# Attention features, a softplus layer and a gated layer in one kernel: two pairs of weight buffers in place of four shared ones, and another pool for the tile y

## The chip, the cores and the metric

The kernel runs on one core of a Trainium2 chip. The metric is device time in microseconds of one execution, the median of the runs shown. The core has five engines that run side by side, each through its own queue in order: TensorE (PE in the profile, its weight loads PEld), VectorE (DVE), ScalarE (ACT), GpSimd (POOL) and SyncE (SP), which here only starts DMAs. They wait for one another by semaphores.

## What is computed

Three layers follow each other, all in float32 (shapes of the reference: batch 4, 8 heads, sequence 576, head size 64, so 2304 tokens of 512):

```python
q_p, k_p = phi(q * scale), phi(k * scale)          # 128 random features each
kv = einsum('bhsm,bhsd->bhmd', k_p, v); z = sum(k_p, axis=2)
x = (q_p @ kv) / (q_p @ z + 1e-6)                  # -> 2304 x 512
h = x @ w_in                                       # 512 -> 2048
g = maximum(h, 0) + log1p(exp(-abs(h)))            # softplus
y = g @ w_out                                      # 2048 -> 512
out = (((y @ w1) * (y @ w2)) @ w3) @ w_out2        # 512 -> 1024 -> 1024 -> 512
```

The five weight matrices come in as 64-bit floats; the kernel makes 32-bit floats of them on the chip, out of the two words of each.

## The kernel before

**Split products.** A float32 product is made of three matmuls of rounded operands (`mm3`, L89): hi by hi, hi by lo and lo by hi, where hi is the rounded value (a copy on ACT) and lo the rest (a subtraction on DVE or POOL). All matmuls are of line L87.

**Stages.** First the attention features (0 to about 150 us). Then *Up1*, the first wide stage (150 to about 341 us): x @ w_in with softplus, in 24 quads. A quad (class `Quad`, L450) is one weight block `win[i]` by one of three groups of 768 tokens; seven products of 384 columns stand for eight, and the sums of operands are made beforehand: s1 to s4 of the tokens (`operands`, L409) and t1 to t4 of the weights (`sum_13`, `sum_2`, `sum_4`). The products are added up by DVE (`add`, L475) out of PSUM, whose banks PE needs again for the next quad: the product with s1 is the third of a quad. Then *pass 1* (about 341 to 598 us): g @ w_out (`down`, L565) in five chunks of tokens (512 four times, then 256), the first two together, so that 16 rows f of w_out times two chunks make 32 steps of 12 matmuls. During pass 1 eight products w3 @ w_out2 are made as well, one each three steps from step 42 on (`fold`). Then *Up2*, the second wide stage, and *pass 2*, the last product.

**The stream of pass 1.** A step m loads `dn` four steps ahead (SP's queue), splits it two steps ahead into `dhi` (ACT, L581) and `dlo` (DVE, L582) and multiplies. At the end of a chunk four accumulators are copied out as `y` (`evict_down`, L614: d = 1, 3 on ACT at L618, d = 0, 2 on DVE at L620), and `store_y` (L732) puts their stores into a list `late`, which `before_1` issues on SP's queue at the start of the next step that isn't the first of a chunk. At the first boundary two chunks end, so there are eight y. Operands `dn`, `dhi`, `dlo` and `y` all come from `mt()`: the pool M_, 14 buffers.

**Weight conversion.** A weight block is a `Job` (L112). Its steps: `load` (DMA on ACT's queue into one of two buffers of L_), `relu` (ACT, L127, takes the buffer f), `floor`, `bits_a`, `bits_b`, `bits_c` (DVE, L130, L136, L143, L150), and then the splits: `hi_` (ACT, L176) and `lo_` (POOL, L181) of f. Blocks with `sums` (w_in and w1/w2) also make t from f (DVE, L157, L160, L163) and split it, `hi_t` (ACT, L189) and `lo_t` (POOL, L193), ahead of f. Four of the w1/w2 blocks are `kept`: their f is stored to DRAM (`spill`, from ACT's queue) in pass 1 and read back in Up2 (`reload`). f, t and the token sums s1 to s4 all come from `tt()`: the pool T_, four buffers under one tag. The splits go to J_ (eight slots) or to X0 and X1, pools of 14 and 28 slots under the tag "x", which hold the token operands of a wide stage (14 per group) and in pass 1 the split w_out blocks (the first 7 in X0, the last 4 in X1, two slots each) and 7 split blocks of w_out2 (X1).

**What sets the order.** Program order is written out by hand: a list `queue` of conversion steps from which `step(rate)` takes some after each product or step of a pass; `need` and `until` take more where PE needs the result. A step that takes slots of J, X0 or X1 waits in the list until the counter `free[pool]` allows it; these counters are bookkeeping in the program text only. The framework then fixes the order of each engine's queue when the program is built: it runs a model of the machine, starts what is ready, program order being the priority (less `URGENT` = 300 for additions, evictions and the stream's splits), and a tile gets a buffer of its pool and tag when one is free in that model. On the chip each engine follows its fixed order and waits where the earlier user of a buffer isn't done.

Of the kernel before, what the change touches and what calls it, by code (L numbers as in the profile page):

```python
# [19 lines left out]
F32 = mybir.dt.float32  # L20
# [24 lines left out]
N = 384  # L45
# [17 lines left out]
def body(ctx: ExitStack, tc: tile.TileContext, q, k, k_rest, v, v_rest, om_t, w_in, w_out, w12, w3, wo, out):  # L63
# [2 lines left out]
    sm = ctx.enter_context(tc.tile_pool(name="sm", bufs=5))  # L66
    M_ = ctx.enter_context(tc.tile_pool(name="M_", bufs=14))
    L_ = ctx.enter_context(tc.tile_pool(name="L_", bufs=2))
    T_ = ctx.enter_context(tc.tile_pool(name="T_", bufs=4))
    J_ = ctx.enter_context(tc.tile_pool(name="J_", bufs=8))  # L70
    dr = ctx.enter_context(tc.tile_pool(name="dr", bufs=1, space=DRAM))
    ps_ = ctx.enter_context(tc.tile_pool(name="ps_", bufs=8, space=PSUM))
# [4 lines left out]
    def mt(n=512, dt=F32, name="m"):  # L77
        return M_.tile([128, n], dt, tag="m", name=name)
# [1 line left out]
    def jt(name):  # L80
        return J_.tile([128, 1024], FR, tag="j", name=name)

    def tt(name):
        return T_.tile([128, 1024], F32, tag="t", name=name)

    def matmul(o, a, b, start, stop, **kw):
        nc.tensor.matmul(out=o, lhsT=a, rhs=b, start=start, stop=stop, **kw)  # L87
# [15 lines left out]
    free = {"J": 8, "X0": 14, "X1": 28}  # L103

    def take(pool, n):
        def ok():
            return free[pool] >= n

        return ok


    class Job:  # L112
# [10 lines left out]
            return self.raw.bitcast(dt).rearrange("p (n w) -> p n w", w=2)[:, :, i]  # L123

        def relu(self):
            self.f = tt("f")[:, :self.n]
            nc.scalar.activation(out=self.f, in_=self.words(1, F32), func=AF.Relu, scale=-1.0)  # L127

        def floor(self):
# [23 lines left out]
            )  # L153

        def sum_13(self):
            self.t = tt("t")
            nc.vector.tensor_tensor(out=self.t[:, 0:512], in0=self.f[:, 256:768], in1=self.f[:, 0:512], op=ALU.subtract)  # L157

        def sum_2(self):
# [6 lines left out]
            nc.scalar.dma_start(out=self.kept, in_=self.f)  # L166

        def reload(self):
            self.f = tt("f")
            nc.sync.dma_start(out=self.f, in_=self.kept)  # L170

        def hi_(self):
# [69 lines left out]
    def until(done):  # L242
        while not done():
            assert pump_one()
# [161 lines left out]
    def xslot(pool, n, dt, name):  # L406
        return pools[pool].tile([128, n], dt, tag="x", name=name)

    def operands(c, src, pool):  # L409

        o, a, s = {}, [], {}

        def load(kk):
            def op():
                r = L_.tile([128, 2, 2 * N], F32, tag="l", name="xq")
                nc.sync.dma_start(out=r, in_=src[:, 2 * kk:2 * kk + 2, 2 * N * c:2 * N * (c + 1)])
                a.append([r[:, :, 0:N], r[:, :, N:2 * N]])
            return op

        def total(name, x, y, op_):  # L420
            def op():
                s[name] = tt(name)[:, 0:2 * N].rearrange("p (k t) -> p k t", k=2)
                nc.vector.tensor_tensor(out=s[name], in0=x(), in1=y(), op=op_)
            return op

        def parts(name, x):
            def op_hi():
                free[pool] -= 2
                o[name] = [xslot(pool, 2 * N, FR, f"x{name}{w}").rearrange("p (k t) -> p k t", k=2) for w in "hl"]
                nc.scalar.copy(out=o[name][0], in_=x())  # L430

            def op_lo():
                nc.vector.tensor_tensor(out=o[name][1], in0=x(), in1=o[name][0].bitcast(F32), op=ALU.subtract)

            return [(op_hi, take(pool, 2)), op_lo]

        a11, a21 = lambda: a[0][0], lambda: a[0][1]
        a12, a22 = lambda: a[1][0], lambda: a[1][1]
        ops = [load(0), load(1)]
        ops += parts("a11", a11)  # L440
        ops += [total("s1", a21, a22, ALU.add), total("s2", lambda: s["s1"], a11, ALU.subtract)]
        ops += parts("s2", lambda: s["s2"])
        ops += [total("s3", a11, a21, ALU.subtract)]
        ops += parts("s3", lambda: s["s3"]) + parts("s1", lambda: s["s1"]) + parts("a12", a12)
        ops += [total("s4", a12, lambda: s["s2"], ALU.subtract)]
        ops += parts("a22", a22) + parts("s4", lambda: s["s4"])
        ops.append(lambda: ready.add(c))
        return o, ops
# [89 lines left out]
    def widen(kind, jobs, after, before_last):  # L538
        n = len(jobs)
        order = [(0, 0), (1, 0), (0, 1), (0, 2), (1, 1), (1, 2)]  # L540
        order += [(i, c) for i in range(2, n - 2) for c in range(NC)]
        order += [(n - 2, 0), (n - 2, 1), (n - 1, 0), (n - 1, 1), (n - 2, 2), (n - 1, 2)]
        last_i, last_c = {i: m for m, (i, c) in enumerate(order)}, {c: m for m, (i, c) in enumerate(order)}
        quads = {}
        for m in range(len(order) + 1):
            if m < len(order):
                i, c = order[m]
                until(lambda: c in ready and jobs[i].done)
                quads[m] = kind(i, c, FIRST_RATE if m < 4 else UP_RATE)
                quads[m].begin()  # L550
            if m == len(order) - 1:
                before_last()
            if m:
                quads.pop(m - 1).finish()
                i, c = order[m - 1]
                if last_i[i] == m - 1:
                    free["J"] += 4
                if last_c[c] == m - 1:
                    free["X0" if c == 0 else "X1"] += 14
                    after(c)  # L560
# [51 lines left out]
        yield  # L612

    def evict_down(d, src, n, name):  # L614
        o = mt(n, name=name)
        with tc.high_priority(URGENT):
            if d % 2:
                nc.scalar.copy(out=o, in_=src)  # L618
            else:
                nc.vector.tensor_copy(out=o, in_=src)  # L620
        return o
# [82 lines left out]
    for s in range(NW):  # L704
        n = min(WB, NF * 512 - WB * s)
# [26 lines left out]
    def store_y(d, t0, n, src):  # L732
        y = evict_down(d, src, n, "y")
        late.append(lambda: nc.sync.dma_start(out=yd[:, d, t0:t0 + n], in_=y))
# [24 lines left out]
            queue.extend(job_ops(wout))  # L759

    widen(Up1, win, after_1, lambda: next(d1))
    ready.clear()
    for x, f in zip(w12_k, wf[KEEP:]):
        x.kept = f
# [4 lines left out]
    next(d1)  # L769
    while late:  # L770
        late.pop(0)()
    for x in wout:
        if x not in given:
            free[x.pool] += 2
# [29 lines left out]
    def store_out(d, t0, n, src):  # L804
        nc.sync.dma_start(out=out[128 * d:128 * d + 128, t0:t0 + n], in_=evict_down(d, src, n, "o"))
# [77 lines left out]
```

## Time and profile before

| | before |
|---|---|
| median of 3 runs | 881.78 us (880.67 to 882.65) |
| the profiled execution | 882.83 us |
| its span, first to last instruction | 881.0 us |
| PE busy | 850.9 us (97%), 5496 matmuls |
| DVE / ACT / POOL busy | 597.6 / 381.8 / 177.9 us |
| mean granted TensorE clock | 0.994 |
| DMA | 141.68 MB, mean 161 GB/s |

A profile is of one execution. Start times are in us from the first instruction. In a timeline row the columns are start, duration, engine, line, operation, out<-in, shape and count; in brackets stands how long the engine had been idle before it and what ended that. The granted clock is a share of 2.4 GHz. Of the profiled execution 1.8 us lie outside its span.

### The profile page before, as it was taken

To read this page: it belongs to the slowest core of one execution; us is meant where nothing else is said; L and a number is where in the kernel's file an instruction comes from. 1 tells how busy PE (TensorE), PEld (TensorE's weight loads), DVE (VectorE), ACT (ScalarE), POOL (GpSimd) and SP (SyncE) were. 2 spreads that over 40 slices of the span, in tenths; PEclk is the share of its full clock that TensorE was granted. 3 is DMA by queue.
4 is the path that set the end of the run, shared out by engine and by line. 5 is a ranking of instruction groups with operands and counts; after the bars stand their busy time and mean duration, and the time that the engine had idled before them with its cause. 6 is when DMAs were issued, how large, how long until landed. Compare 5 with 4: busy or idle time off the path is not lost.

```text
span 881.0 us, 14617 instructions
## 1 busy us (share of the span) xinstructions
PE 850.9 (97%) x5496; PEld 763.9 (87%) x5496; DVE 597.6 (68%) x932; ACT 381.8 (43%) x796; POOL 177.9 (20%) x110
## 2 busy tenths in 40 slices
PE   8999989999899999999989999999999999999998
PEld 7888878989899988788768888899999999988887
DVE  5678788888775587887986686169986655563322
ACT  6678978563443455444433332164321111132221
POOL 3524420022222243222311211100042222000000
PEclk9999999999999999999989999999999999999999
DMA  8623534565443457766676664064322211364432
GB/s 298 240 84 97 156 99 133 186 215 181 156 149 133 150 195 266 239 190 237 203 275 235 238 219 161 31 204 137 126 102 78 78 54 55 128 201 144 143 120 96
DMA packets 72535, 141.68 MB, mean 161 GB/s; under 512 B 7056, under 2 KB 39952, under 8 KB 69392
## 3 DMA queue, kind: packets, MB, share of 16 engines
q1 hardware_dynamic: 65984, 102.99, 35.0%
q10 hardware_dynamic: 6480, 37.75, 12.5%
q8 instruction: 43, 0.70, 0.3%
q14 instruction: 28, 0.23, 0.1%
HBM read 94.05 MB, written 46.66 MB: 160 GB/s over the span
## 4 chain that ended last, share of the span: by engine, by line
PE 53%; DVE 4%; DMA 2%; issue 1%; ACT 1%; POOL 0%; ACTq 0%; DVEq 0%; POOLq 0%
PE ps L87 53%; DMA raw<-in_w 1%; DVE f L150 1%; DMA dn<-gd 1%; DVE f L143 1%; DVE dlo L582 0%; DVE f L130 0%; DMA raw<-in_wo 0%; DVE f L136 0%; ACT dhi L581 0%; DVE c L475 0%; DVE u L475 0%; ACT hi L176 0%; POOL tlo L193 0%; ACT f L127 0%
## 5 line engine op out<-in xcount | busy, mean ns | idle before, releaser
L181 POOL TENSOR_TENSOR lo<-f,hi 128x512 fp32r<-128x512 f32 (+3 forms) x58 | 93.2, 1621 | 195.1 <-ACT hi L176 162.5
L582 DVE TENSOR_TENSOR dlo<-dn,dhi 128x512 fp32r<-128x512 f32 (+1 forms) x120 | 89.0, 752 | 62.6 <-ACT dhi L581 44.1
L87 PE MATMUL ps<-dlo,hi 128*128 128x512 f32 (+1 forms) x320 | 120.8, 378 | 4.8 <-DVE dlo L582 4.8
L87 PE MATMUL ps<-dhi,hi 128*128 128x512 f32 (+1 forms) x320 | 119.1, 375 | 1.2 <-DVE c L475 0.7
L87 PE MATMUL ps<-dhi,lo 128*128 128x512 f32 (+1 forms) x320 | 120.2, 376 | 0.0
L193 POOL TENSOR_TENSOR tlo<-t,thi 128x1024 fp32r<-128x1024 f32 x16 | 39.7, 2478 | 301.6 <-ACT thi L189 195.5
L581 ACT CAST dhi<-dn 128x512 fp32r<-128x512 f32 (+1 forms) x120 | 67.3, 577 | 65.5 <-DVE dlo L582 30.7
L87 PEld LDWEIGHTS ps<-dlo,hi 128*128 128x128 f32 x320 | 60.8, 190 | 17.7 <-DVE dlo L582 6.2
L130 DVE SCALAR_TENSOR_TENSOR f<-raw,f 128x1024 f32<-128x1024 f32 (+2 forms) x43 | 51.0, 1188 | 33.2 <-ACT f L127 33.0
L87 PEld LDWEIGHTS ps<-dhi,hi 128*128 128x128 f32 x320 | 60.5, 189 | 14.6 <-DVE c L475 1.8
L475 DVE TENSOR_TENSOR c<-ps,u 128x384 f32<-128x384 f32 x144 | 71.6, 550 | 0.9
L87 PEld LDWEIGHTS ps<-dhi,lo 128*128 128x128 f32 x320 | 60.9, 190 | 11.7
L482 ACT COPY p<-ps 128x384 f32<-128x384 f32 x48 | 22.9, 477 | 103.8 <-PE ps L87 99.1
L475 DVE TENSOR_TENSOR u<-ps,p 128x384 f32<-128x384 f32 x48 | 26.6, 555 | 60.8 <-PE ps L87 60.8
L127 ACT ACTIVATE f<-raw 128x1024 f32<-128x1024 f32 (+2 forms) x43 | 42.5, 993 | 49.7 <-DMA raw<-in_w 25.4
L176 ACT CAST hi<-f 128x1024 fp32r<-128x1024 f32 (+2 forms) x42 | 38.5, 922 | 57.6 <-PE ps L87 30.8
L507 ACT ACTIVATE c<-c 128x384 f32<-128x384 f32 x72 | 35.2, 524 | 63.3 <-DVE c L475 59.0
L309 DVE TENSOR_REDUCE nmax<-ps 128x4 f32<-128x512 f32 x72 | 48.2, 683 | 19.4 <-PE ps L87 10.0
L87 PE MATMUL ps<-dlo,w34h 128*128 128x512 f32 (+1 forms) x160 | 59.6, 373 | 0.0
L87 PE MATMUL ps<-dhi,w34l 128*128 128x512 f32 (+1 forms) x160 | 59.6, 373 | 0.0
L87 PE MATMUL ps<-dhi,w34h 128*128 128x512 f32 (+1 forms) x160 | 59.1, 373 | 0.0
L150 DVE SCALAR_TENSOR_TENSOR f<-raw,f 128x1024 int32<-128x1024 int32 (+2 forms) x43 | 53.1, 1236 | 0.6
(147 smaller groups left out, 2163.5 us busy)
## 6 DMA issues: line engine op xcount, KB each, us to landing
gd<-c SPq DMA_DIRECT2D x96, 192.0 KB, 2.4
dn<-gd SPq DMA_DIRECT2D x64, 256.0 KB, 3.6
raw<-in_w ACTq DMA_DIRECT2D x16, 1024.0 KB, 6.0
pd<-c SPq DMA_DIRECT2D x48, 192.0 KB, 1.9
dn<-pd SPq DMA_DIRECT2D x32, 256.0 KB, 3.2
raw<-in_w_out ACTq DMA_DIRECT2D x10, 768.0 KB, 4.1
raw<-in_w_in ACTq DMA_DIRECT2D x6, 1024.0 KB, 5.0
rawq<-in_q SPq DMA_DIRECT2D x18, 256.0 KB, 3.8
```

Source lines behind the costliest of these rows:

```text
L87: nc.tensor.matmul(out=o, lhsT=a, rhs=b, start=start, stop=stop, **kw)
L127: nc.scalar.activation(out=self.f, in_=self.words(1, F32), func=AF.Relu, scale=-1.0)
L130: nc.vector.scalar_tensor_tensor(out=self.f, in0=self.words(1, F32), scalar=SMALLEST, in1=self.f, op0=ALU.max, op1=ALU.max)
L150: nc.vector.scalar_tensor_tensor(out=fi, in0=self.words(0, I32), scalar=29, in1=fi, op0=ALU.logical_shift_right, op1=ALU.bitwise_or,)
L176: nc.scalar.copy(out=self.hi, in_=self.f)
L181: nc.gpsimd.tensor_tensor(out=self.lo[:, a:b], in0=self.f[:, a:b], in1=self.hi[:, a:b].bitcast(F32), op=ALU.subtract)
L193: nc.gpsimd.tensor_tensor(out=self.tlo, in0=self.t, in1=self.thi.bitcast(F32), op=ALU.subtract)
L309: nc.vector.tensor_reduce(out=nmax, in_=pj, axis=AX.X, op=ALU.max, negate=True)
L475: nc.vector.tensor_tensor(out=z, in0=bank, in1=y, op=ALU.add)
L507: nc.scalar.activation(out=dst, in_=src, func=AF.Softplus)
L581: nc.scalar.copy(out=hi, in_=got[m])
L582: nc.vector.tensor_tensor(out=lo, in0=got.pop(m), in1=hi.bitcast(F32), op=ALU.subtract)
```

## The change

T_ has two buffers under each of two tags in place of four under one: f takes "f", t takes "t"; of the token sums s1 and s3 take "f", s2 and s4 "t". At the end of a chunk of pass 1 y is allotted in X1, not in M_; the outputs of pass 2 stay in M_. The counter of X1 is lowered by 6 after Up1 and raised by 6 after pass 1.

```diff
-    T_ = ctx.enter_context(tc.tile_pool(name="T_", bufs=4))
+    T_ = ctx.enter_context(tc.tile_pool(name="T_", bufs=2))
...
-    def tt(name):
-        return T_.tile([128, 1024], F32, tag="t", name=name)
+    def tt(name, tag):
+        return T_.tile([128, 1024], F32, tag=tag, name=name)
...
         def relu(self):
-            self.f = tt("f")[:, :self.n]
+            self.f = tt("f", "f")[:, :self.n]
...
         def sum_13(self):
-            self.t = tt("t")
+            self.t = tt("t", "t")
...
         def reload(self):
-            self.f = tt("f")
+            self.f = tt("f", "f")
...
         def total(name, x, y, op_):
             def op():
-                s[name] = tt(name)[:, 0:2 * N].rearrange("p (k t) -> p k t", k=2)
+                s[name] = tt(name, "f" if name in ("s1", "s3") else "t")[:, 0:2 * N].rearrange("p (k t) -> p k t", k=2)
...
     def evict_down(d, src, n, name):
-        o = mt(n, name=name)
+        o = xslot("X1", n, F32, name) if name == "y" else mt(n, name=name)
...
     widen(Up1, win, after_1, lambda: next(d1))
+    free["X1"] -= 6
     ready.clear()
...
     next(d1)
     while late:
         late.pop(0)()
+    free["X1"] += 6
```

## Rows read from the trace of the kernel before

**Rows 1.** The page: its span, and the engines' busy time with the share of the span.

```profile
span 881.0 us, 14617 instructions
...
PE 850.9 (97%) x5496; PEld 763.9 (87%) x5496; DVE 597.6 (68%) x932; ACT 381.8 (43%) x796; POOL 177.9 (20%) x110
```

**Rows 2.** Windows: length, busy PE, PEld, DVE, ACT, POOL, granted clock, DMA share, GB/s.

```profile
150.00:345.00 195.00, 182.91 (x1021) 178.95 (x1022) 147.02 (x221) 93.85 (x167) 48.00 (x25) 0.99 0.52 176
345.00:445.00 100.00, 95.05 (x404) 75.06 (x402) 83.95 (x101) 46.85 (x74) 26.49 (x16) 0.99 0.69 225
...
450.00:500.00 50.00, 50.00 (x216) 40.28 (x215) 37.32 (x39) 16.60 (x24) 5.63 (x2) 1.00 0.61 210
```

**Rows 3.** Timeline of PE: the five matmuls with over 1.5 us of idle before them.

```profile
230.08 0.45 PE L87 MATMUL ps<-xs1h,thi 128*128 128x384 f32 x1 [2.30 <-DVE c L475]
...
263.07 0.44 PE L87 MATMUL ps<-xs1h,thi 128*128 128x384 f32 x1 [1.55 <-DVE c L475]
...
287.13 0.44 PE L87 MATMUL ps<-xs1h,thi 128*128 128x384 f32 x1 [1.95 <-DVE c L475]
...
311.16 0.44 PE L87 MATMUL ps<-xs1h,thi 128*128 128x384 f32 x1 [1.92 <-DVE c L475]
...
444.95 0.79 PE L87 MATMUL ps<-dlo,hi 128*128 128x512 f32 x1 [4.30 <-DVE dlo L582]
```

**Rows 4.** Timeline of ACT, 253 to 284 us: relus that had waited for POOL.

```profile
253.35 1.13 ACT L127 ACTIVATE f<-raw 128x1024 f32<-128x1024 f32 x1 [1.60 <-POOL tlo L193]
...
277.24 0.90 ACT L127 ACTIVATE f<-raw 128x768 f32<-128x768 f32 x1 [1.60 <-POOL tlo L193]
...
283.32 0.90 ACT L127 ACTIVATE f<-raw 128x768 f32<-128x768 f32 x1 [3.07 <-POOL lo L181]
```

**Rows 5.** Timeline of POOL, 256 to 284 us: the splits "lo" of two w_in blocks.

```profile
256.72 3.84 POOL L181 TENSOR_TENSOR lo<-f,hi 128x256 fp32r<-128x256 f32 x2 [3.40 <-ACT hi L176]
...
280.38 2.90 POOL L181 TENSOR_TENSOR lo<-f,hi 128x256 fp32r<-128x256 f32 x2 [3.17 <-ACT hi L176]
```

**Rows 6.** Timeline of DVE, 278 to 288 us: conversion and additions of one round.

```profile
278.17 0.96 DVE L130 SCALAR_TENSOR_TENSOR f<-raw,f 128x768 f32<-128x768 f32 x1 [2.69 <-ACT f L127]
...
280.75 1.38 DVE L150 SCALAR_TENSOR_TENSOR f<-raw,f 128x768 int32<-128x768 int32 x1
...
284.25 0.96 DVE L130 SCALAR_TENSOR_TENSOR f<-raw,f 128x768 f32<-128x768 f32 x1 [1.65 <-ACT f L127]
...
286.06 1.48 DVE L475 TENSOR_TENSOR c<-ps,u 128x384 f32<-128x384 f32 x3
```

**Rows 7.** Timelines of DVE, ACT and SP at the first boundary of pass 1.

```profile
432.79 0.68 DVE L620 COPY y<-ps 128x512 f32<-128x512 f32 x1
...
438.05 2.99 DVE L130 SCALAR_TENSOR_TENSOR f<-raw,f 128x1024 f32<-128x1024 f32 x1
...
444.21 1.28 DVE L582 TENSOR_TENSOR dlo<-dn,dhi 128x512 fp32r<-128x512 f32 x2
...
438.28 1.14 ACT L581 CAST dhi<-dn 128x512 fp32r<-128x512 f32 x2
...
442.26 6.53 SPq L574 DMA_DIRECT2D dn<-gd  x5
```

**Rows 8.** DMA issues: queue, count, KB each, median us from issue to landing.

```profile
wf<-f ACTq DMA_DIRECT2D x4, 512.0 KB, 6.8
...
yd<-y SPq DMA_DIRECT2D x16, 256.0 KB, 5.8
```

**Rows 9.** Windows again (columns as in Rows 2): the end of Up1, and after the boundary.

```profile
313.00:345.00 32.00, 31.25 (x174) 29.87 (x174) 26.68 (x39) 17.17 (x31) 14.07 (x7) 1.00 0.67 224
...
445.00:450.00 5.00, 5.00 (x12) 3.94 (x13) 3.39 (x4) 3.11 (x5) 2.37 (x1) 0.50 0.93 336
```

**Rows 10.** Timelines of ACT and POOL in pass 1: a relu, and the next split.

```profile
469.45 1.13 ACT L127 ACTIVATE f<-raw 128x1024 f32<-128x1024 f32 x1 [4.25 <-DMA raw<-in_w]
...
475.78 2.40 POOL L181 TENSOR_TENSOR lo<-f,hi 128x1024 fp32r<-128x1024 f32 x1 [27.90 <-ACT hi L176]
```

## The prediction

> **What bounds the kernel now.** I read the engines' busy time first: PE (TensorE) is busy 850.9 of 881.0 us, DVE 68%, ACT 43% [rows 1]. The time is therefore PE's own work and the holes in it. A table by stage says where holes are: in 150 to 345 us PE is busy 182.91 of 195, in 345 to 445 us 95.05 of 100, while 450 to 500 us is full at 216 matmuls, 0.2315 us apart [rows 2]. Third, PE's timeline. The reader should see five holes over 1.5 us [rows 3]: four in the first wide stage (Up1), all before the first product of "s1" and all ended by the DVE line that adds the partial products (L475), and one of 4.30 us at 444.95 in the first narrow pass, ended by "dlo" (L582).
>
> What stands behind the holes is read from the engines that run late. In Up1 the weight conversion and PE's additions share DVE's queue, which runs in order. At 253.35 ACT's relu, which opens the buffer of a weight block, had waited 1.60 us for POOL's "tlo"; at 277.24 the same again; at 283.32 it waited 3.07 us for POOL's "lo" [rows 4]; the pair returns at 301.28 and 307.35. Both are waits for a buffer of the pool T_: POOL was still reading the values or the sums in it. "lo" ended at 256.72 + 3.84 = 260.56 and at 280.38 + 2.90 = 283.28 [rows 5]. DVE's floor, next after the relu, then idles 2.69 and 1.65 us, and the additions behind it start at 286.06 [rows 6], so PE waits 1.95 us at 287.13. The hole at 230.08 has no T_ wait behind it, and I leave it.
>
> At 440.65 (444.95 less 4.30) PE has finished the first two chunks and needs the operand "dlo" of the third. Its "dhi" began at 438.28, yet "dlo" ran at 444.21, behind a floor of 2.99 us and more conversion; meanwhile "dn" loads went out from 442.26 only [rows 7]. All of dn, dhi, dlo and the eight y tiles come from the 14 buffers of M_: four dn ahead, one in use and three pairs make eleven, which leaves three for eight y; each y gives its buffer back when its store has landed, 5.8 us after issue in the median [rows 8]. That is a buffer wait, and the order of DVE was fixed around it.
>
> **Part 1: T_ in two pairs.** No instruction is added or removed; only who waits for what. In Up1 blocks take f and t alternately. Before, a new f took whichever of four buffers came free, the t of the block before: free at "tlo". After, it takes the f of the block before last, free at "lo". So the waits for "tlo" go, and the relu comes later, by at most 260.56 - 253.35 = 7.2 us in the first round and 283.32 - 277.24 = 6.1 us in each of the next two [rows 4, 5]. Each round keeps one relu that waits for "lo" and loses one that waited for "tlo".
>
> The three holes of 1.55, 1.95 and 1.92 us make 5.42 us [rows 3]. Per round 2.69 us of DVE idle go and 1.65 us stay [rows 6]; 2.69 is more than the hole, so the hole would close if the additions moved up by it; but the wait that stays is next to them. Ends: 5.42 us gained, and nothing. I take 4.4, leaving about 0.35 us per hole, since the larger wait is the one that goes. A loss here is the second rival.
>
> The lookahead shrinks: before, four w_out blocks were converted to values ahead of 313 us (relus from 277.24 to 307.35); with two f buffers it is two. One block's conversion on DVE ran from 278.17 to 280.75 + 1.38 = 282.13, 4.0 us [rows 6]. So 8 us move behind 313 us, where DVE has 32 - 26.68 = 5.3 us free up to 345 [rows 9], and the rest falls in pass 1, where 100 - 83.95 = 16 us are free [rows 2]. PE's own additions and splits have priority 300 over conversions when the order is made. A w_out block is due every 1.5 steps of 24 matmuls, 8.3 us, from 345 us on. Cost: nothing; without that cover 2.7 us, at most 8.
>
> In pass 1 only f is in use, so two buffers stand where four stood. The relu at 469.45 would now wait for the "lo" that ended at 475.78 + 2.40 = 478.18 [rows 10], 8.7 us later; a spilled block holds its f until its store has landed, 6.8 us [rows 8]. These blocks feed products that come one per three steps, so I cost this at nothing. If ACT's order put such a relu ahead of a "dhi", 8.7 us would stand against a lead of two steps of 12 matmuls, 2 x 2.78 = 5.6 us: 3.1 us per event. The sums before the second wide stage (Up2) alternate too; their splits wait for X0 slots that pass 1 returns only in its last chunk, so a later sum costs nothing there.
>
> **Part 2: y into X1.** During pass 1 X1 holds 8 tiles of w_out and 14 of w_out2, so 6 of 28 are empty; the counter lowered by 6 keeps the planner of the queue off them. Nobody else wants them: the second operand group needs 14, which the last fold returns. The eight y of the first boundary need two tiles more than six; the first y was written at 432.79 [rows 7], and 0.71 + 5.8 us later, near 439.3, its slot is back; the last two y are written near 437.5, so two evictions may wait about 2 us, on DVE and ACT, ahead of later splits. The stores and loads on SP's queue stay the same in number; the dn loads no longer stand behind y's landing. Gain: the hole of 4.30 us, and the half clock after it. From 445 to 450 us the granted clock was 0.50 (1.2 of 2.4 GHz), with 12 matmuls in 5 us [rows 9]; 12 x (0.417 - 0.2315) = 2.2 us. Together 6.5 us; ends 6.5 and 0. DVE is nearly full there, so I keep 0.6 us of hole and take 5.9. Later boundaries have four y each and show no hole over 1.5 us: no gain, no loss.
>
> **The sum.** 4.4 + 5.9 = 10.3 us off. The profiled execution took 882.83 us (a span of 881.0 and 1.8 around it), 1.05 above the median of 881.78. 882.83 - 10.3 = 872.5 in its terms, 871.5 as a median. PE is full after 450 us, so what is saved ahead of it should reach the end.
>
> **A rule that speaks against it.** What the rows show: three holes of 1.55 to 1.95 us, some 24 us apart [rows 3], behind waits for T_ [rows 4]. The Trainium skill, Perfetto Trace Analysis, section Identifying the Most-Contended Engine, says that a gap which repeats on the engine that should be saturated can mean too little room for the next tile, buffer count among the causes. By that reading f, which goes from a choice of four buffers to two, would lengthen the holes, and the sum would turn from a gain into a loss. By the rows the buffers are enough and are only handed out in the wrong order. The trace of before cannot settle it, so it is a rival.
>
> **Rivals.** First, only y pays: the additions in Up1 are held by the "lo" wait that stays, and holes of the old size form around it. For it: that wait is the longer one, 3.07 against 1.60 us. Against: DVE's idle in front of its floor was the shorter one. 881.78 - 5.9 = 875.9.
>
> Second, two f buffers are too few. Place: Up1 from 253 us on. If DVE's order keeps each floor ahead of the additions, each now 7.2, 6.1 and 6.1 us later, the holes grow by up to 19.4 us, against 5.9 gained: up to 895.3. From 5.9 + 1.8 = 7.7 us of such holding on, it is slower than before. Against it: the order is made knowing which buffer is taken, so floors should sink behind additions. It would be near 885.
>
> Third, y gains nothing: the hole at 440.65 is DVE's conversion load and not M_, or the two last y hold the splits. For it: DVE has almost no idle from 430 to 445 us. 881.78 - 4.4 = 877.4.
>
> Fourth, the change does not act: other buffer waits re-form at both places and cancel, 881 to 883.
>
> **How the numbers follow.** Forecast 0.53; only y 0.20; only T_ 0.08; no change 0.07; too few f buffers 0.12. Faster by over 0.2% (1.8 us, about what a measurement of this kernel can tell from none): 0.53 + 0.20 + 0.08 = 0.81; same 0.07; slower 0.12. The forecast's own range is 868 to 875. The low end of the whole is 881.78 - 11.9 = 869.9 with both parts in full, less the 2.30 us hole at 230.08, should the new order close it: 867. The high end takes in both single-part rivals with 2 us of lost cover: 879.5. Outside are the slower cases and part of no change.
>
> **What would show it.** Right: no relu in Up1 waits for "tlo"; the holes before "s1" between 250 and 315 us are under 0.5 us; "dlo" of the third chunk runs within 2 us of its "dhi"; the clock stays at 1.0 from 430 to 455 us; y is written without a wait for a store. Wrong: DVE's floor idle over 4 us before an addition, an ACT relu with a "dhi" behind it in pass 1, or a new hole in PE between 313 and 440 us.

## The result, and the profile after

The changed kernel takes 891.83 us (median of 9 runs, 883.92 to 895.38) against 881.78 us for the kernel before in the same set of runs (9 runs, 878.92 to 884.71). The ratio is 1.0103 with an interval of 1.0079 to 1.0127: it is slower by 1%, and the forecast of 871.5 us with a range of 867.0 to 879.5 us was wrong, in sign too. The profiled execution of after took 883.92 us and is the fastest of the nine; a second profile, further down, lies nearer the median. Two runs of the sets that follow stand far above all others of their kernel (1025.63 us of y alone, 2098.64 us of before) and are left out of the ratios.

The page says little. The span is 882.1 us where it was 881.0, and PE, ACT and POOL are busy for nearly the same times, DVE for 7 us less [rows 1]:

```profile
span 882.1 us, 14591 instructions
...
PE 850.0 (96%) x5496; PEld 762.3 (86%) x5496; DVE 590.2 (67%) x932; ACT 381.9 (43%) x796; POOL 177.9 (20%) x110
```

The stages say more. Windows of after (columns as in Rows 2):

```profile
150.00:345.00 195.00, 188.06 (x1043) 181.29 (x1042) 143.77 (x217) 96.30 (x172) 46.12 (x26) 1.00 0.54 186
345.00:445.00 100.00, 100.00 (x430) 80.49 (x430) 62.59 (x87) 38.93 (x64) 17.69 (x11) 1.00 0.57 182
445.00:600.00 155.00, 146.83 (x720) 123.53 (x719) 107.62 (x122) 59.41 (x88) 32.72 (x15) 0.98 0.60 201
...
568.00:585.00 17.00, 10.81 (x66) 9.92 (x65) 15.85 (x15) 7.30 (x13) 11.15 (x6) 0.80 0.39 129
615.00:626.00 11.00, 6.40 (x19) 5.23 (x20) 7.66 (x10) 6.05 (x8) 0.00 (x0) 0.69 0.29 97
```

and the one window of before that is not among Rows 2:

```profile
445.00:600.00 155.00, 154.72 (x750) 129.01 (x751) 95.79 (x114) 55.82 (x88) 21.61 (x11) 0.98 0.54 184
```

The gain that was forecast is there. From 150 to 345 us PE is busy 188.06 us for 182.91, from 345 to 445 us it is full for 95.05 [rows 2], with 430 matmuls for 404. From 445 to 600 us it does 720 matmuls for 750: the gain is given back there, in 17 us at the end of pass 1 in which PE is busy for 10.81 and DVE for 15.85, and once more at 615 us, in Up2.

Matmuls come in nearly the same order in both kernels, so the start of PE's n-th matmul in one trace against that in the other shows where time is gained and lost (us ahead of before, each from one profile; the last two columns are kernels of the experiments):

| matmul | before starts it at | after | after, second profile | pairs alone | whole change, w_out2 ahead of y |
|---|---|---|---|---|---|
| 1800 (attention features) | 146.57 | 4.2 | 3.6 | 3.8 | 3.6 |
| 2900 (first steps of pass 1) | 353.58 | 10.2 | 7.9 | 9.6 | 9.8 |
| 3600 (behind the first boundary) | 524.75 | 16.2 | 11.9 | 16.3 | 17.7 |
| 3800 | 571.38 | 16.5 | 12.1 | 16.3 | 17.7 |
| 4200 (in Up2) | 632.14 | -1.9 | -7.3 | 15.9 | 17.7 |
| 5496 (last) | 877.65 | -1.1 | -6.7 | 14.9 | 16.6 |

After is 16.5 us ahead at the 3800th matmul, more than the whole forecast, and behind at the 4200th. Between these two PE is idle for 11.4 us more than in before, and busy for 7.0 us more over the same 400 matmuls, as part of them ran at a lower clock. What happened in between is read backwards from PE. Its timeline, the holes over 1.2 us behind 440 us, save one of 1.67 us at 576.06, which a `dlo` ended too:

```profile
460.42 0.50 PE L87 MATMUL ps<-hi,lo 128*128 128x512 f32 x1 [1.58 <-POOL lo L181]
...
572.64 0.38 PE L87 MATMUL ps<-dlo,hi 128*128 128x256 f32 x1 [2.76 <-DVE dlo L582]
...
617.71 0.45 PE L87 MATMUL ps<-xs2h,thi 128*128 128x384 f32 x1 [3.23 <-ACT xs2h L430]
...
621.97 0.69 PE L87 MATMUL ps<-xs3h,thi 128*128 128x384 f32 x1 [1.30 <-ACT xs3h L430]
```

Behind each of the two places the granted clock is at its lower level, 1.2 GHz, for 6.8 us (574.11 to 580.93, 618.49 to 625.31); in before it is 1.00 throughout both places, with 115 matmuls from 568 to 585 us for the 66 here. DVE's timeline shows why `dlo` was late, and xs2h; one split of POOL stands below it:

```profile
563.60 0.42 DVE L582 TENSOR_TENSOR dlo<-dn,dhi 128x256 fp32r<-128x256 f32 x1
...
568.88 1.22 DVE L150 SCALAR_TENSOR_TENSOR f<-raw,f 128x1024 int32<-128x1024 int32 x1
570.02 2.57 DVE L582 TENSOR_TENSOR dlo<-dn,dhi 128x256 fp32r<-128x256 f32 x1
572.51 1.21 DVE L157 TENSOR_TENSOR t<-f 128x512 f32<-128x512 f32 x1
573.65 2.02 DVE L433 TENSOR_TENSOR xa11l<-xq,xa11h 128x768 fp32r<-128x768 f32 x1
...
580.60 1.49 DVE L423 TENSOR_TENSOR s<-xq 128x768 f32<-128x768 f32 x1
...
614.10 1.82 DVE L423 TENSOR_TENSOR s<-xq 128x768 f32<-128x768 f32 x2
615.84 0.95 DVE L423 TENSOR_TENSOR s<-s,xq 128x768 f32<-128x768 f32 x1
```

```profile
568.92 3.38 POOL L193 TENSOR_TENSOR tlo<-t,thi 128x1024 fp32r<-128x1024 f32 x1 [15.14 <-ACT thi L189]
```

In the last chunk of pass 1, whose steps are half as long, DVE still converts the last w1/w2 blocks (L150, and L157, their sums t) while it already splits operands for Up2 (L433). In before the same last conversion and its sum ran at 535.37 and 537.11, and the first token sum (L423) at 540.96, 40 us earlier than the 580.60 here. The `dlo` at 570.02 was also slow. It ran beside POOL's split of such a late block and took 2.57 us; two more of its shape beside such splits (578.22 and 582.01) took 2.46 and 1.49, and the other 21 took 0.41 to 0.43, as did all 24 in before. At 0.42 us it would have ended 2.15 us sooner, most of the hole of 2.76 us (an estimate from these rows). So the late blocks cost the last chunk twice: by DVE's own steps for them, and by the steps that run beside POOL's splits of them. The conversions were late because ACT's relus were; of ACT's timeline:

```profile
501.96 1.14 ACT L127 ACTIVATE f<-raw 128x1024 f32<-128x1024 f32 x1 [3.18 <-DMA wf<-f]
...
519.15 1.14 ACT L127 ACTIVATE f<-raw 128x1024 f32<-128x1024 f32 x1 [4.64 <-DMA wf<-f]
...
537.00 1.14 ACT L127 ACTIVATE f<-raw 128x1024 f32<-128x1024 f32 x1 [3.15 <-DMA wf<-f]
```

Each opens the buffer f of a block and waits until the spill of the block before last (`wf<-f`) has landed. Before had no such wait: its last two relus of these blocks stand at 521.60 and 526.31, those of after at 554.67 and 559.82. But the three waits make 10.97 us of 33, or of some 50 when the 16.5 us that PE is ahead are counted. The rest is older. POOL's timeline, and ACT's beside it:

```profile
375.96 1.29 POOL L181 TENSOR_TENSOR lo<-f,hi 128x512 fp32r<-128x512 f32 x1 [2.01 <-ACT hi L176]
424.36 2.53 POOL L181 TENSOR_TENSOR lo<-f,hi 128x512 fp32r<-128x512 f32 x2 [47.10 <-ACT hi L176]
```

```profile
379.00 0.69 ACT L127 ACTIVATE f<-raw 128x512 f32<-128x512 f32 x1 [0.54 <-DMA raw<-in_wo]
...
421.78 0.59 ACT L618 COPY y<-ps 128x512 f32<-128x512 f32 x1 [0.81 <-PE ps L87]
423.18 0.59 ACT L618 COPY y<-ps 128x512 f32<-128x512 f32 x1 [0.81 <-PE ps L87]
423.66 1.14 ACT L176 CAST hi<-f 128x512 fp32r<-128x512 f32 x2
425.68 0.67 ACT L127 ACTIVATE f<-raw 128x512 f32<-128x512 f32 x1 [0.88 <-POOL lo L181]
```

No weight block is split for 47.10 us (in before the longest such pause of POOL between 360 and 440 us is 10.17 us), and no relu opens one from 379.00 to 425.68. The two blocks in hand are of w_out2 and were finished as values at 381.62 and 383.41 (DVE's last step on them began at 380.93 and 382.72, 0.69 us each). Their `hi` goes into slots of X1, and runs right behind ACT's last copy of y of the first boundary. Slots of X1 are given out in program order, and y is asked for at the boundary, ahead in program order of the third to the seventh w_out2 block (the eighth takes no slots of X1, but stands behind them in the list). Only four w_out and two w_out2 blocks, 12 slots of 28, come before it. Conversion running ahead would have taken up the others some 40 us sooner. So nobody holds these slots and nobody may have them; both buffers f are held by blocks that wait; and behind them wait all later conversions.

### The profile page after: what moved, and what is told of

The parts are those of the page before. It is cut to its first block, busy times and chain, and to the rows that moved or that the text cites. A ratio compares the mean times of both kernels' runs of the same rounds, so it can differ in the third digit from the quotient of the medians.

```text
span 882.1 us, 14591 instructions
## 1 busy us (share of the span) xinstructions
PE 850.0 (96%) x5496; PEld 762.3 (86%) x5496; DVE 590.2 (67%) x932; ACT 381.9 (43%) x796; POOL 177.9 (20%) x110
## 4 chain that ended last, share of the span: by engine, by line
PE 75%; DVE 11%; issue 5%; DMA 4%; POOL 2%; ACT 2%; SPq 0%; ACTq 0%; DVEq 0%; POOLq 0%
PE ps L87 73%; POOL lo L181 2%; DVE s L423 1%; DMA xq<-xd 1%; PE ps L368 1%; DVE f L150 1%; DVE c L475 1%; DVE u L475 1%; DVE f L143 1%; DVE f L130 1%; PE ps L398 1%; DMA raw<-in_w_out 1%; ACT f L127 1%; DMA raw<-in_w 1%; DVE dlo L582 1%
## 5 line engine op out<-in xcount | busy, mean ns | idle before, releaser
L582 DVE TENSOR_TENSOR dlo<-dn,dhi 128x512 fp32r<-128x512 f32 (+1 forms) x120 | 86.7, 728 | 85.4 <-PE ps L87 48.0
L130 DVE SCALAR_TENSOR_TENSOR f<-raw,f 128x1024 f32<-128x1024 f32 (+2 forms) x43 | 48.3, 1122 | 52.1 <-ACT f L127 51.8
L475 DVE TENSOR_TENSOR c<-ps,u 128x384 f32<-128x384 f32 x144 | 71.5, 549 | 0.8
L475 DVE TENSOR_TENSOR u<-ps,p 128x384 f32<-128x384 f32 x48 | 26.7, 556 | 60.1 <-PE ps L87 57.9
L127 ACT ACTIVATE f<-raw 128x1024 f32<-128x1024 f32 (+2 forms) x43 | 42.9, 997 | 45.1 <-DMA raw<-in_w 13.5
L309 DVE TENSOR_REDUCE nmax<-ps 128x4 f32<-128x512 f32 x72 | 48.4, 684 | 18.4 <-PE ps L87 8.6
```

Source lines behind the costliest of these rows:

```text
L130: nc.vector.scalar_tensor_tensor(out=self.f, in0=self.words(1, F32), scalar=SMALLEST, in1=self.f, op0=ALU.max, op1=ALU.max)
L309: nc.vector.tensor_reduce(out=nmax, in_=pj, axis=AX.X, op=ALU.max, negate=True)
L475: nc.vector.tensor_tensor(out=z, in0=bank, in1=y, op=ALU.add)
L582: nc.vector.tensor_tensor(out=lo, in0=got.pop(m), in1=hi.bitcast(F32), op=ALU.subtract)
```

## The experiments

The theory after this reading: the lost time is not in either part but in the order of requests for X1, and it is made worse by two f buffers. Rivals: two buffers f are too few by themselves (waits for spills); the move of y costs by itself.

**Each part alone.** The pairs with y left in M_ (`bufs=2` and the tags as in the change):

```diff
-    def tt(name):
-        return T_.tile([128, 1024], F32, tag="t", name=name)
+    def tt(name, tag):
+        return T_.tile([128, 1024], F32, tag=tag, name=name)
...
     def evict_down(d, src, n, name):
         o = mt(n, name=name)
```

> The change without its second part: T_ in two pairs, y from M_ as before. Theory A (the changed kernel loses because the splits of five w_out2 blocks take their X1 slots in program order, behind the eight y): nothing blocks them here, so no pause of ACT's and POOL's splits between 383 and 424 us; the holes before the products with s1 at 263, 287 and 311 us gone; 870 to 879 us, faster than before. Theory B (two f buffers are too few for the spilled blocks): the relus that wait for a spill stay, the conversion runs late into Up2, 887 us or more.

Measured: 868.19 us (863.08 to 868.91, 4 runs), 0.9836 of before (0.9792 to 0.9879), a gain of 13.0 us on the 881.15 of that set, and below the range of either theory. Of pass 1's end and of the boundary its windows and its timeline of PE show:

```profile
445.00:600.00 155.00, 154.07 (x779) 131.44 (x778) 107.72 (x134) 59.55 (x91) 22.12 (x11) 1.00 0.56 186
```

```profile
447.32 0.50 PE L87 MATMUL ps<-dlo,hi 128*128 128x512 f32 x1 [0.52 <-DVE dlo L582]
```

The boundary's hole is 0.52 us in place of 4.30 [rows 3], although y still comes from M_. Its relus wait for spills too, four times and 10.7 us together, and it costs nothing: the last one starts at 525.1. So the rival "two buffers are too few" falls as it stood.

The move of y with the four shared buffers (T_ as before; the two lines of the counter as in the change):

```diff
-        o = mt(n, name=name)
+        o = xslot("X1", n, F32, name) if name == "y" else mt(n, name=name)
```

> The change without its first part: T_ four shared buffers, y from X1 with the counter lowered by 6. Theory A: five w_out2 splits stand behind the four y of ACT at the first boundary as in the changed kernel, a pause of some 40 us in POOL, conversion late, holes in the last chunk of pass 1 and at the start of Up2: 884 to 895 us. Theory B: with four f buffers the conversion keeps up: 873 to 878 us.

Measured: 884.36 us (median of 10; nine of them 881.80 to 886.36), 1.0035 (1.0015 to 1.0055): slower by 3.2 us. The pause is there, and the end of pass 1 has a hole of 2.14 us at 581.42; the one at 617 is absent. POOL's timeline:

```profile
437.04 4.25 POOL L181 TENSOR_TENSOR lo<-f,hi 128x512 fp32r<-128x512 f32 x3 [54.05 <-ACT hi L176]
```

**The order alone.** The whole change, and the w_out2 blocks asked for ahead of the first y in the program's text, in `before_1`:

```diff
+        if m == 2 * NF - 2:
+            for x in wo_j:
+                need(x)
         if m in FOLD_AT:
```

> The whole change, but in program order all steps of the eight w_out2 blocks are taken from the list before step 30 of pass 1, thus before the first y. Theory A: the splits take their X1 slots before any y, the pause is gone, both gains of the prediction stay (about 4 us in Up1, about 6 us at the first boundary): 866 to 874 us. Theory B: two f buffers still hold the conversion back behind the spills: 884 us or more.

Measured: 866.01 us (864.84 to 868.99, 4 runs), 0.9828 (0.979 to 0.9867), 15.1 us less than before and 26 less than the change. The same buffers, the same instructions; POOL's long pause is gone, and PE is full to 600 us. POOL's timeline, then the windows:

```profile
383.43 1.48 POOL L181 TENSOR_TENSOR lo<-f,hi 128x512 fp32r<-128x512 f32 x1 [5.23 <-ACT hi L176]
386.19 1.29 POOL L181 TENSOR_TENSOR lo<-f,hi 128x512 fp32r<-128x512 f32 x1 [1.28 <-ACT hi L176]
393.58 1.35 POOL L181 TENSOR_TENSOR lo<-f,hi 128x512 fp32r<-128x512 f32 x1 [6.10 <-ACT hi L176]
```

```profile
445.00:600.00 155.00, 154.88 (x785) 132.70 (x785) 108.83 (x134) 58.78 (x91) 21.60 (x11) 1.00 0.55 191
```

It is the best version together with the pairs alone: their runs overlap, and with the pairs in place the move of y, well ordered, is worth 2 us by the medians, which is not told from nothing.

The same order with T_ as before:

> T_ four shared buffers, y from X1, the w_out2 blocks taken from the list before step 30. Theory A: no pause, the hole of 4.3 us at the first boundary gone and the holes in Up1 as in the kernel before: 873 to 878 us. Theory B says the same here; if it comes out above 882 us, moving y costs by something else than the order of the slots.

Measured: 878.26 us (10 runs), 0.9952 (0.9934 to 0.997), just above the range named: the move of y is worth 2.9 us where its order is right. The boundary keeps 0.90 us of its 4.30, and the holes of Up1 stay, 3.04 us at 230.44 and three of 1.57 to 1.92.

**The change once more**, for the spread of its runs:

> The changed kernel once more, for a second profile and its time beside the others on this chip. Both theories: 887 to 895 us; the profile, if it falls on a longer execution than the first, should show its extra time between 560 and 640 us (end of pass 1, start of Up2) and nowhere else.

Measured: 891.85 us (887.33 to 893.93, 7 runs), 1.0091 (1.0063 to 1.0119); the profile is of 889.45 us. It loses 19.4 us between the 3800th and 4200th matmul (12.1 ahead, then 7.3 behind), as the first profile loses 18.4. But it has lost time earlier as well, which was not expected: the two profiles part at 172 us. Windows of the changed kernel, the first profile and the second:

```profile
172.00:178.00 6.00, 5.71 (x33) 5.50 (x33) 6.00 (x8) 3.58 (x5) 0.00 (x0) 1.00 0.14 35
```

```profile
172.00:178.00 6.00, 5.61 (x21) 5.28 (x22) 4.95 (x6) 4.04 (x6) 0.00 (x0) 0.72 0.09 27
```

Both have the same hole of 1.30 us ahead of this (at 171.65 and at 172.10), and in one execution the clock fell behind it while in the other it did not. In the second it fell once more at 463.50, behind a hole of 2.17 us at 463.23; the hole at that place in the first, 1.58 us at 460.42, had no such sequel.

**Four f in two tags.** Is it the number of f buffers, or who shares with whom? Tags given out in turn: two pairs still, but a run of f alone, as in pass 1, has all four.

```diff
     def tt(name, tag):
+        turn[0] += 1
+        tag = "ab"[turn[0] % 2]
         return T_.tile([128, 1024], F32, tag=tag, name=name)
```

With y in X1, late in program order:

> The changed kernel, but the two tags of T_ are given out in turn to every request, whatever it is for: in Up1 that is f and t as in the change, in pass 1, where only f is asked for, all four buffers serve f. y still from X1, splits still behind it. Theory A2 (the pause of 40 us is made dear by the two f buffers, which are both held by blocks that wait behind y, and after that by spills): 868 to 879 us. Theory B2 (the pause costs what it does whatever the number of f buffers): 885 us or more.

Measured: 878.96 us (874.78 to 884.32, 10 runs), 0.9962 (0.993 to 0.9994). POOL pauses 54.03 us, longer than in the change, and the time is 13 us lower. With y in M_:

> T_ given out in turn, y from M_ as before. Theory A2: the gain of T_ in two pairs comes from f not standing behind t in one row of requests, which is the same here: 863 to 872 us, as with the pairs alone (868.2). Rival: the gain came from fewer conversions being let ahead (two f in place of four): then Up1's holes come back and it is 874 us or more.

Measured: 876.75 us (871.71 to 877.4, 6 runs), 0.9924 (0.9891 to 0.9956). That missed the theory's number and met the rival's. In PE's timeline two holes of Up1 are back (one shown), and that of the boundary whole:

```profile
280.23 0.45 PE L91 MATMUL ps<-xs1h,thi 128*128 128x384 f32 x1 [1.92 <-DVE c L479]
...
438.49 0.50 PE L91 MATMUL ps<-dlo,hi 128*128 128x512 f32 x1 [4.27 <-DVE dlo L586]
```

So a part of the pairs' gain is not "the right buffer in turn", as I had argued, but goes with fewer f buffers for a run of blocks. What ACT's relus show of it: with tags in turn two w_out blocks are opened 6 us apart ahead of each hole (270.4 and 276.4, then 294.4 and 300.5), with the pairs alone one at 271.5 and one at 293.8. That DVE, which runs in order, then has fewer conversions between PE's additions fits this, but was not tested by itself. With y in X1 and w_out2 first:

> T_ given out in turn, y from X1, the w_out2 blocks taken from the list before step 30. Theory A2: nothing waits behind y, so four or two f buffers make little difference: 862 to 871 us (866.0 with pairs by kind). Rival as for the run before: 874 us or more.

Measured: 871.34 us (869.24 to 872.04, 4 runs), 0.9858 (0.9816 to 0.99), with the holes of Up1 at 278.60 and 302.84 (1.72 us each); the range named was missed by 0.3 us.

**A third f.** The last set tests the share of the two f buffers by itself. Three f need 4 KB more per partition, which are taken from M_: it goes from 14 to 12 buffers in all four kernels; the lines of TF are in the two with a third f.

```diff
-    M_ = ctx.enter_context(tc.tile_pool(name="M_", bufs=14))
+    M_ = ctx.enter_context(tc.tile_pool(name="M_", bufs=12))
     T_ = ctx.enter_context(tc.tile_pool(name="T_", bufs=2))
+    TF = ctx.enter_context(tc.tile_pool(name="TF", bufs=3))
...
-        return T_.tile([128, 1024], F32, tag=tag, name=name)
+        return (TF if tag == "f" else T_).tile([128, 1024], F32, tag=tag, name=name)
```

The change with 12 buffers of M_, then with a third f (y late in both):

> The whole change with M_ cut from 14 buffers to 12, as the control for the runs with three f buffers (which need that room). M_ holds no y now; four loads ahead, one in use and three pairs of splits make eleven, so both theories expect the change's own time within about 4 us: 888 to 896. Above 900 would mean that 12 buffers are too few and the set tells little.

> As the control, but three buffers for f (two for t as before). Theory: with two f buffers both are held by blocks that wait behind y, and spills in series keep the backlog; a third f lets conversions go on beside a spill, so the penalty of the late order shrinks to what it was with shared or alternating buffers (6 to 8 us over its early counterpart), a time near 874 to 882, with the last two relus of the w1/w2 blocks some 10 us or more earlier than the 554.67 and 559.82 us of the change. Rival: the number of f buffers in pass 1 has no part and the order alone makes the loss: within 3 us of the control.

Measured: 893.24 us (889.49 to 896.24, 4 runs; 1.0125, 1.0066 to 1.0184), so M_ does not matter, and 873.88 us (872.26 to 875.07, 8 runs; 0.9904, 0.9876 to 0.9931) with the third f: 19.4 us less. POOL's pause is no shorter. POOL's timeline with three f:

```profile
428.17 4.26 POOL L182 TENSOR_TENSOR lo<-f,hi 128x512 fp32r<-128x512 f32 x3 [54.56 <-ACT hi L177]
```

What ended ACT's idle time before its relus from 480 us on (releaser: us, times), first with two f, then with three:

```profile
  DMA wf<-f: 12.2, 3
  DMA raw<-in_w: 6.6, 5
```

```profile
  DMA raw<-in_w: 2.7, 3
  DVE f L151: 2.2, 1
```

No relu waits for a spill any more. The last one stands at 552.7 against 567.1 in the control, 14.4 us earlier. Against the change's 559.82, which the expectation named, it is only 7 us, so that number was missed. Yet windows from 445 to 600 us, two f above three, show what it is worth to PE (the first is of an execution of 896.24 us, the slowest of its four, the second of 874.00):

```profile
445.00:600.00 155.00, 145.32 (x679) 119.96 (x678) 106.91 (x120) 59.41 (x86) 35.01 (x16) 0.96 0.59 199
```

```profile
445.00:600.00 155.00, 150.57 (x750) 126.72 (x749) 129.78 (x136) 66.60 (x96) 35.32 (x15) 1.00 0.63 211
```

Both again with the w_out2 blocks ahead of y:

> The whole change with the w_out2 blocks ahead of y in program order, M_ cut to 12. Both theories: within about 4 us of the 866.01 us of the same with 14 buffers, 863 to 870.

> The same with three buffers for f. Theory (conversions let too far ahead crowd the additions in the first wide stage): with a third f one more block goes ahead and holes before the s1 products in 250 to 315 us come back in part (at least one over 1 us), 868 to 874. Rival (two f buffers are merely enough and a third can only help or do nothing): no such hole, 863 to 867, not slower than the control.

Measured: 867.16 us (864.79 to 872.41, 4 runs; 0.9846, 0.9776 to 0.9917) and 868.62 us (867.65 to 869.69, 4 runs; 0.9848, 0.9798 to 0.9899). The times do not tell them apart. The timeline of PE does in part: with three f one hole ahead of s1 has grown, from 0.81 us at 315.28 in the control to 1.82, just outside the stretch I had named.

```profile
316.53 0.45 PE L88 MATMUL ps<-xs1h,thi 128*128 128x384 f32 x1 [1.82 <-DVE c L476]
```

The set as a table (medians in us; before 881.2 to 882.3 in its sets, M_ of 12 where marked):

| T_ | y in M_ | y in X1, as the change has it | y in X1, w_out2 first | cost of the late order |
|---|---|---|---|---|
| four shared | 881.15 | 884.36 | 878.26 | 6.1 |
| two pairs, tags in turn | 876.75 | 878.96 | 871.34 | 7.6 |
| f three, t two (M_ 12) | | 873.88 | 868.62 | 5.3 |
| f two, t two (M_ 12) | | 893.24 | 867.16 | 26.1 |
| f two, t two | 868.19 | 891.83 | 866.01 | 25.8 |

The late order costs 5 to 8 us with any T_ that lets three f stand side by side, and 26 with two. That is the answer: neither the order nor the two f buffers alone make the change slower than before by 1%, but both at once. With a third f the pause of POOL stays and the waits for spills go.

What two f add is seen where the last conversion falls. Against before's clock the last relu of y alone (562.70) is even later than the change's (559.82), but PE has come 13 us less far there. Against PE's own work the order is plain (one profile each; `bits_c` of the last block against the first matmul of the last chunk, and what was lost on before between matmuls, in us):

| late order, with | last chunk from | last `bits_c` | lies | lost, 3800th to 3900th matmul | lost, 3900th to 4200th |
|---|---|---|---|---|---|
| two f (the change) | 553.99 | 568.88 | 14.9 behind | 4.9 | 13.5 |
| two f, M_ 12 | 561.37 | 576.11 | 14.7 behind | 5.5 | 16.6 |
| four shared | 572.09 | 571.33 | 0.8 ahead | 6.0 | -0.2 |
| tags in turn | 561.4 | 557.95 | 3.4 ahead | 7.9 | -1.1 |
| three f | 563.13 | 559.64 | 3.5 ahead | 3.4 | 0.0 |

The loss at the end of pass 1 comes with the late order whatever T_ is. With two f the last blocks are converted inside the last chunk, the operands of Up2 come behind them, and 13 to 17 us more are lost there.

## Why the prediction was wrong

**The pairs in Up1 (4.4 us): right, and too small.** No relu of Up1 waits for "tlo" any more; between 230 and 345 us four wait for POOL's "lo", 5.1 us together. From 230 us on the holes before s1 are gone but for 0.53 us at 314.98, and the hole at 230.08, which I left out, went too. A new one stands earlier, where I had not looked for a loss: 2.05 us at 203.48, ahead of a22. The relu at 194.59 had waited 5.47 us for "lo", and the `bits_c` behind it (199.78) took 3.17 us beside a split of POOL. The lookahead I had wrong: four relus of w_out stand ahead of 313 us in after as in before (270.98, 293.21, 303.76, 306.19), not two; only their spacing changed. By the table of matmuls Up1 gave 6.0 us in after (4.2 to 10.2). Another 4.2 us came from the attention stage, which I had not looked at. They belong to the pairs: the two kernels that only move y are 0.1 and 0.4 us behind at the 1800th matmul. The relu of the second w_in block starts there at 48.20 in place of 69.69, its f having a tag of its own; that this makes the gain was not tested. (A sixth hole over 1.5 us, which rows 3 leave out, 1.72 us at 151.06 ahead of a transposition, is still there in after, 1.52 us at 146.67.)

**"In pass 1 only f is in use ... I cost this at nothing": the step that failed, with the next.** I weighed a late f against the product that it feeds, one per three steps, and against a "dhi" behind it on ACT. What stands behind it is the list of conversions itself, which is taken in order: a block that is late makes all later ones late, down to the last sums and the operands of Up2, which are due when DVE has the short steps of the last chunk. The waits for spills that I named ("holds its f until its store has landed, 6.8 us") came, 3.15 to 4.64 us each. With the pairs alone they do no harm, and on top of the late order they do. What I put at nothing, with the slots of X1 below, measured 25.8 us (891.83 against 866.01 with w_out2 first), and 19.4 of such a loss go with a third f.

**"6 of 28 are empty ... Nobody else wants them": false.** I counted slots and not the order in which they are asked for. Five blocks of w_out2 that need X1 come after y in the program's text, and they were to be converted ahead of it. The counter lowered by 6 is not what holds them: it acts on the list of conversion steps only, and the program without its two lines has the same instructions in the same order on every queue (read from the built program; not run). The two last y were to wait about 2 us for a store. In after they don't, as the slots of those blocks are empty. Where w_out2 goes first they do: 2.07 us on DVE at 427.25 and 2.80 us on ACT at 427.87, with no hole in PE.

**y out of M_ (5.9 us): right in place, too large, and only half the cause.** With T_ as before and w_out2 first, the boundary gave 4.1 us by the matmuls (1.4 behind at the 3200th, 2.6 ahead at the 3600th), and the median 2.9. "That is a buffer wait" holds in part. The hole needs both y in M_ and four blocks of lookahead: 4.27 us with both (tags in turn), 0.52 with y in M_ and two f, 0.90 with y in X1 and four f. So the third rival, DVE's conversion load, had a part as well, and the two gains could not be added. A part of that load was not the conversion itself: the floor of 2.99 us at 438.05 [rows 7] ran beside a split of POOL (437.55, 2.41 us), and the 19 floors of its shape with none beside them took 1.21 to 1.23. With the order put right the whole change gains 15.1 us where the sum had 10.3. That the two are near is in part luck: 3.6 us of the 15.1 come from the attention stage, which is not in the sum.

**"PE is full after 450 us, so what is saved ahead of it should reach the end": wrong.** I read PE's fullness as a fact of the stage. It was full because conversions ran far enough ahead. The stretch where my change could empty it, the last chunk and the first quads of Up2, was not read.

**The rule set against the change.** The rule cited in the prediction (the Trainium skill, Perfetto Trace Analysis; it stands there under Optimization Strategy, the section behind the one that I named) would have the repeated holes lengthen with fewer buffers. From 230 us on in Up1 the trace disagrees: with two f the holes closed, and with a third one of 0.81 us grew to 1.82 (the one at 203.48 went the rule's way, 2.05 us with two f, 1.61 and 1.50 with three). In pass 1 it agrees: a third f gave 19.4 us.

**The rivals.** "Two f buffers are too few" (0.12) had the sign and half of the cause. I put it into Up1 from 253 us on, where it was not, and priced it up to 895.3 us for reasons that did not occur. The wrong signs that I named, a new hole between 313 and 440 us or a long idle of DVE's floor, were not those that came; "an ACT relu with a dhi behind it in pass 1" was nearest, as the relus did wait there.

**What stays open.** How much of the pairs' gain is lookahead and how much the order of hand-out: pairs and tags in turn are 8.6 us apart, but they differ in more than the number of f. What the slow `dlo` of the last chunk and the lower clock each cost was not taken apart by a run. Whether the order of requests could be kept and slots reserved for w_out2 in another way was not tried.

## What to carry to other kernels

Before a new tenant is put into empty slots, list who asks for them later in program order, and whether the work that asks is done ahead of its time: empty now and free for the taking are two things. A stage in which the bottleneck engine is full may be full because something else runs far ahead, so follow a change of buffers to the last user of the list that they feed, not to the next product, and measure lateness against the bottleneck engine's work, not against the clock on the wall. And when two changes meet in one supply, run each alone and both: 13.0 us gained and 3.2 lost became 10 lost.

## What the runs showed of the chip that was not expected

**DVE beside POOL.** In after the 307 conversion steps, sums and splits of DVE (all but L136) that ran with POOL idle took no more than 1.2 times the median of their line and shape. Of the 49 that ran beside a split of POOL for over 0.3 of their length 27 took longer than that, and the 49 took 33 us more than such medians in all. Of the additions out of PSUM (L475) 43 ran so, and none took longer. In before it is 34 us; what the change moved is where they fall.

**The clock.** The granted clock can part two executions of one program. Behind the same 1.30 us hole near 172 us it stayed at 1.00 once and fell to the lower level another time, with 33 matmuls in 6 us and then 21. Eleven of the profiles here have this hole, and it fell behind it in three. The second execution of the change is 2.2 us behind the first by the 2900th matmul and 4.3 by the 3600th. The runs of the change, with its holes, spread by 11 us (883.92 to 895.38, 9 runs), those of the best version, with nearly none, by 4 (864.84 to 868.99, 4 runs). What decides whether the clock falls is not shown here.
